# Attention and two feed-forward layers: earlier transposes of two tiles, three warming products, another spread of the feed-forward steps

## The chip, the cores and the metric

One NeuronCore of a Trainium2 chip runs the whole program. The metric is the device time of one execution in microseconds (us). It was taken in three runs of the kernel before; one further execution was recorded by the hardware profiler, and the rows below come from that one.

## The reference

For 2 batches and 12 heads, 448 positions and a head size of 64, the program computes causal attention, lays the heads side by side to 896 tokens of 768 features, and sends these through two feed-forward layers of width 2048:

```python
scores = where(mask, -1e9, q @ k.T / sqrt(64))
attn = exp(scores - max(scores))
attn = attn / (sum(attn) + 1e-9)
x = attn @ v                                   # 896 x 768
h = x @ w_in;  x = (max(h, 0) + alpha * min(h, 0)) @ w_out
h = x @ w2_in
g = where(h >= 1, h, where(h <= -1, 0, (h + 1) ** 2 / 4))
out = g @ w2_out
```

## The kernel before

**Attention.** The 24 head sequences are worked on as 12 pairs, numbered from 0. The 448 rows of scores of each head are cut into three tiles of 128 rows (tile i has 128 * (i + 1) columns, since the mask cuts the rest) and a rest of 64 rows; the rests of both heads share one tile of 128 partitions ("rest tile", index NQ). A pair goes through three periods of a loop over p: in period p the scores, the reductions, the exponentials and the normalization of pair p are issued, the transposes of pair p - 1, and the product with V of pair p - 2. There are 14 periods, so that the last two only finish pairs 10 and 11.

The work of one pair: `scores` (lines 376 and 372) puts products into the PSUM banks s0 and s1 (one for each head) and s2 (rest tile). VectorE reads them (line 383), adds the mask, takes the row's extreme and writes the tile to SBUF. `expo` (line 392) makes the exponentials on ScalarE, in place. `norm` divides: GpSimd adds 1e-9 to the sums (line 399), VectorE takes the reciprocal (line 400), GpSimd multiplies the tiles (line 403), in the order 0, 1, rest, 2. `transp` (line 430) turns 64 x 64 blocks by products with the identity into the PSUM banks t0 and t1, each of which exists twice, so that a third group of transposes has to wait until the first is copied out. The copies to SBUF (line 439) are shared: of tiles 0 to 2 ScalarE copies one head and VectorE the other; of the rest tile VectorE copies both. `attnv` (lines 446 and 454) multiplies with V into the one bank o, from which ScalarE takes a rounded part (`high`, line 213) and VectorE the remainder (`low`, line 216).

**Order.** It is written out by hand: the schedule is the order in which the loop body issues (lines 489 to 529), and each engine works its queue in that order. The banks s0 and s1 exist once: the third tile's scores wait until the first two tiles' scores are read, and the next pair's first scores wait until the third tile's are read.

**Loads.** SyncE's queue issues nearly all transfers in program order: per pair the queries and keys (line 336, 448 KB; those of pair 0 in two halves, one of them on ScalarE's queue, line 334), two small blocks of queries for the rest tile (line 340), and seven pieces of V (line 348). In period 1 two chunks of the first feed-forward weights (line 103, 768 KB each) are issued ahead of the loads for pair 3 that follow in period 2.

**Before the attention.** `warm_up` (line 72) issues NWARM = 9 products of zeros, 512 columns each, into the bank o, one after the other.

**Feed-forward.** Weights come as 64-bit numbers. `Weights.prime` is a generator that splits the first three chunks into two parts of reduced precision, one step at each call: a magnitude on ScalarE (line 113), four steps on VectorE, the last of them with a cast on ScalarE (line 150), a subtraction on VectorE (line 153), and then the next load and magnitude. `early_tiles` is a generator that issues products of the first feed-forward layer (line 253) for tiles of the input that are ready: its ten steps have six products each for the first output tile, three each for the second, over five of the six input tiles; the first output tile uses the banks s0 and s1. `spare(n)` calls both at three places of a period: one step of `prime` at the first place from period 3 on, and in the last two periods one step of `prime` and two steps of `early_tiles` at each place. What is then left of both runs after the loop; the four passes of the feed-forward layers (`run_layer`) follow.

Of the kernel before, what the change touches and what calls it, by code (L numbers as in the profile page):

```python
# [22 lines left out]
def attention_moe_moe_kernel(ctx: ExitStack, tc: tile.TileContext, qk, v, w1, w2, w3, w4, alpha, out):  # L23
# [8 lines left out]
    nc = tc.nc  # L32
# [13 lines left out]
    NM, NC2, _, KC, _ = w2.shape  # L46
    SCALE = 1.0 / float(D) ** 0.5
    MASK = -1e9 / SCALE
    NWARM = 9

    const = ctx.enter_context(tc.tile_pool(name="const", bufs=1))
    xpool = ctx.enter_context(tc.tile_pool(name="x", bufs=1))
# [4 lines left out]
    def f32(t):  # L57
        return t.bitcast(F32)
# [7 lines left out]
    def warm_up():  # L66

        z = const.tile([128, 512], F32R, tag="zero", name="zero")
        nc.vector.memset(f32(z), 0.0)  # L69
        for _ in range(NWARM):  # L70
            ps = ps_o.tile([128, 512], F32, tag="o", name="warm_ps")
            nc.tensor.matmul(ps, lhsT=z[:, :128], rhs=z, start=True, stop=True)  # L72

    def constants():
        nc.vector.memset(half, 0.5)
        make_identity(nc, ident)
        for t, p0, n in ((mask, 0, Q), (mask_rest, 0, D), (mask_rest, D, D)):
            if p0 == 0:
                nc.gpsimd.memset(t, 0.0)
            d = t[p0:p0 + n, t.shape[1] - n:]  # L80
            nc.gpsimd.affine_select(
                out=d, in_=d, compare_op=ALU.is_ge, fill=MASK, base=0, pattern=[[-1, n]], channel_multiplier=1
            )


    class Weights:
# [82 lines left out]
        def next(self):  # L169
            self.n_used += 1  # L170
            return self.split.pop(self.n_used - 1)
# [59 lines left out]
    def interleave(a, b):  # L231
        a, b = list(a), list(b)
        while a or b:
            for ops in (a, b):
                if ops:
                    ops.pop(0)()

    def new_banks():

        pools = (ps_s, "s0"), (ps_s, "s1"), (ps_s, "s2"), (ps_o, "o"), (ps_t, "t0"), (ps_t, "t1"), (ps_t, "t0"), (ps_t, "t1")  # L240
        while True:
            for pool, tag in pools:
                yield pool.tile([128, 512], F32, tag=tag, name="ps")
# [17 lines left out]
    def early_tiles(batches):  # L261

        for f, bs in enumerate(batches):
            ws = wts.next()
            ps = {b: new_tile() for b in bs}
            early[f] = ws, ps
            for k in range(KD - 1):
                products(ps, ws, x_t, k, k, k == 0, False)
                yield
# [35 lines left out]
    class Attention:  # L305
# [101 lines left out]
        def transp(self, p, tiles):  # L407


            ps = [self.ps_t.tile([128, 512], F32, tag=f"t{h}", name=f"t{h}_ps") for h in range(2)]  # L410
            if 0 in tiles:

                self.pt[p] = (
                    self.ap.tile([Q, 2, 2, NQ, NQ * D], F32, tag="pt", name="pt", bufs=2),
                    self.ap.tile([Q, 2, NC, D], F32, tag="pt_rest", name="pt_rest", bufs=2),
                )
            (pt, pt_rest), off, copies = self.pt[p], 0, []
            for i in tiles:
                n = NC if i == NQ else i + 1
                rows = self.rows(p, i)  # L420
                dst = [
                    t[:, off:off + len(rows) * n * D].rearrange("p (j c q) -> p j c q", c=n, q=D) for t in ps
                ]
                off += len(rows) * n * D
                for c in range(n):
                    for j, (e, _) in enumerate(rows):
                        e = self.prest[p % 3] if i == NQ else e
                        for h in range(2):
                            g = slice(h * D, (h + 1) * D)
                            nc.tensor.transpose(dst[h][:, j, c, :], e[g, c * Q:(c + 1) * Q], ident[g, g])  # L430
                if i == NQ:

                    for h in range(2):
                        copies.append((nc.vector.tensor_copy, pt_rest[:, h], dst[h][:, 0]))
                else:
                    for h, copy in enumerate((nc.scalar.copy, nc.vector.tensor_copy)):
                        copies.append((copy, pt[:, h, :, :n, i * D:(i + 1) * D], dst[h]))
            for copy, to, src in copies:
                copy(to, src)  # L439
# [23 lines left out]
    with tc.manual_schedule():  # L463
        wts = Weights()
        ps_s, ps_t, ps_o = (
            ctx.enter_context(tc.tile_pool(name=f"ps_{n}", bufs=b, space=PSUM))
            for n, b in (("s", 1), ("t", 2), ("o", 1))
        )
        banks = new_banks()
        with ExitStack() as pa:  # L470
            ap = pa.enter_context(tc.tile_pool(name="attn", bufs=2))
            at = Attention(ap, ps_s, ps_t, ps_o)
            at.zeros()
            at.load(0)
            warm_up()
            at.load(1)
            at.load_v(0)
            nc.sync.dma_start(out=alpha_sb, in_=alpha)
            constants()
            early = {}  # L480
            fill = early_tiles(((0, 1), (0,)))
            prime = wts.prime()
            PRIME = 3

            for p in range(NP + 2):
                new, mid, old = p < NP, 1 <= p <= NP, p >= 2  # L490

                def spare(n):
                    if p >= PRIME and (n == 0 or not new):
                        next(prime, None)
                    if not new:
                        next(fill, None)
                        next(fill, None)

                if new:
                    at.scores(p, (0, 1))  # L500
                    at.scores(p, (NQ,))
                    at.expo(p, (0, 1, NQ))
                if old:
                    at.attnv(p - 2)
                    high, low = at.evac(p - 2)
                    high()
                spare(0)
                if new:
                    at.scores(p, (2,))
                if mid:  # L510
                    at.transp(p - 1, (0, 1))
                if old:
                    low()
                if new:
                    at.expo(p, (2,))
                spare(2)
                if mid:
                    at.transp(p - 1, (NQ,))
                    at.transp(p - 1, (2,))
                if new:  # L520
                    at.norm(p)
                spare(1)
                if 0 < p < NP - 1:
                    at.load(p + 1)
                if p + 1 < NP:
                    at.load_v(p + 1)
                if p == PRIME - 2:
                    wts.load()
                    wts.load()
            for _ in fill:  # L530
                pass
            for _ in prime:
                pass
        gpool = ctx.enter_context(tc.tile_pool(name="g", bufs=1))
        ep = ctx.enter_context(tc.tile_pool(name="ep", bufs=2))
        late = []
        for layer in (1, 2, 3, 4):
            late = run_layer(layer, late)
            if layer % 2 == 0:
                interleave(late, [])  # L540
                late = []
# [44 lines left out]
```

## Time and profile before

| | us |
|---|---|
| median of 3 runs | 569.93 |
| lowest, highest | 567.62, 570.9 |
| the profiled execution | 569.33 |
| its span in the profile | 567.4 |

Engines in that span: TensorE's products 550.1 us busy (97%), its weight loads 482.7 (85%), VectorE 420.9 (74%), ScalarE 237.8 (42%), GpSimd 136.1 (24%). TensorE's granted clock is 0.996 of full speed in the mean. The span counts from the first instruction to the last; the profiled execution's own time is 1.9 us longer. In the rows PE is TensorE's products, PEld its weight loads, DVE VectorE, ACT ScalarE, POOL GpSimd and SP SyncE; a q behind a name is the queue's sequencer. L376 is line 376 of the kernel. Busy time of TensorE counts overlapping products once and includes the end of the last one, so it says when work was there and not how dense it was.

### The profile page before, as it was taken

The numbers are of one execution on the slowest core, as the hardware profiler recorded it, in microseconds if no ns is written. First come the engines' busy times: TensorE is split into PE (matmuls) and PEld (weight loads), VectorE is DVE, ScalarE is ACT, GpSimd is POOL, SyncE is SP. The second block draws the span as 40 slices with busy tenths as digits, with TensorE's granted clock in tenths as the row PEclk, the third lists the DMA queues.
The fourth block names the chain that finished last, engine by engine and source line by source line (L and its number), as shares of the span: only waits on it lengthen the run. The fifth ranks groups of instructions, "written<-read, shape, count | busy, mean of one in ns | idle before, by whom it ended". The sixth has DMA issues, their size and how long they took to land.

```text
span 567.4 us, 8740 instructions
## 1 busy us (share of the span) xinstructions
PE 550.1 (97%) x3201; PEld 482.7 (85%) x3201; DVE 420.9 (74%) x809; ACT 237.8 (42%) x497; POOL 136.1 (24%) x179
## 2 busy tenths in 40 slices
PE   8888888999999999999999999999999999999997
PEld 3555556899999999999999999999999999999996
DVE  1778874788888899876665868888888867655750
ACT  2777883233333333332332335555555533232220
POOL 2556653033333333000000003333333300000000
PEclk9999998999999999999999999999999999999999
DMA  4643610333333223445233533333332235434421
GB/s 123 216 125 110 183 31 5 109 111 113 112 111 112 93 75 79 145 113 145 102 89 110 166 113 111 112 111 113 111 94 75 75 119 144 137 118 137 143 71 32
DMA packets 25674, 62.31 MB, mean 110 GB/s; under 512 B 5280, under 2 KB 13984, under 8 KB 25632
## 3 DMA queue, kind: packets, MB, share of 16 engines
q1 hardware_dynamic: 23760, 60.15, 33.7%
q10 hardware_dynamic: 1872, 1.61, 0.8%
q8 instruction: 25, 0.41, 0.3%
q14 instruction: 17, 0.14, 0.1%
HBM read 58.99 MB, written 2.75 MB: 109 GB/s over the span
## 4 chain that ended last, share of the span: by engine, by line
PE 95%; DVE 3%; issue 1%; POOL 1%; ACT 0%; ACTq 0%; POOLq 0%
PE ps L253 82%; PE s_ps L376 3%; PE o_ps L446 3%; PE rest_ps L372 2%; DVE pexp L383 2%; PE warm_ps L72 1%; PE t_ps L430 1%; DVE pt L439 1%; PE o_ps L454 1%; POOL pexp L403 0%; ACT pexp L392 0%; POOL prest L403 0%; DVE x L216 0%; DVE stat L383 0%; DVE zero L69 0%
## 5 line engine op out<-in xcount | busy, mean ns | idle before, releaser
L253 PE MATMUL ps<-x,w_split 128*128 128x448 f32 x1152 | 235.0, 366 | 0.0
L253 PE MATMUL ps<-g,w_split 128*128 128x448 f32 x1152 | 233.8, 365 | 0.0
L253 PEld LDWEIGHTS ps<-x,w_split 128*128 128x128 f32 x1152 | 216.1, 188 | 17.6 <-DVE w_split L153 0.4
L253 PEld LDWEIGHTS ps<-g,w_split 128*128 128x128 f32 x1152 | 216.4, 188 | 17.1
L177 POOL TENSOR_TENSOR g<-act_g,g 128x448 fp32r<-128x448 f32 x64 | 85.6, 1338 | 274.1 <-ACT g L176 274.1
L150 ACT CAST w_split<-w_f 128x512 fp32r<-128x512 f32 (+1 forms) x80 | 56.5, 707 | 126.9 <-DVE w_f L147 94.9
L153 DVE TENSOR_TENSOR w_split<-w_f,w_split 128x512 fp32r<-128x512 f32 (+1 forms) x80 | 66.1, 827 | 50.5 <-ACT w_split L150 50.5
L176 ACT CAST g<-act_g 128x448 fp32r<-128x448 f32 x64 | 36.2, 565 | 76.6 <-DVE act_g L189 62.8
L129 DVE TENSOR_SCALAR w_f<-w_f 128x512 f32<-128x512 f32 (+1 forms) x80 | 58.5, 731 | 8.7 <-ACT w_f L113 8.5
L141 DVE SCALAR_TENSOR_TENSOR w_f<-w_raw,w_f 128x512 uint32<-128x512 uint32 (+1 forms) x80 | 63.5, 793 | 1.4
L147 DVE SCALAR_TENSOR_TENSOR w_f<-w_raw,w_f 128x512 uint32<-128x512 uint32 (+1 forms) x80 | 63.5, 793 | 1.4
L113 ACT ACTIVATE w_f<-w_raw 128x512 f32<-128x512 f32 (+1 forms) x80 | 61.2, 765 | 0.5 <-DMA w_raw<-w 0.4
L392 ACT ACTIVATE pexp<-pexp,stat 128x128 f32<-128x128 f32 (+2 forms) x72 | 35.9, 501 | 18.3 <-DVE stat L383 18.3
L383 DVE CUSTOM_DVE_ANT_0 pexp<-s_ps,mask 128x128 f32<-128x128 f32 (+2 forms) x72 | 26.2, 412 | 22.6 <-PE s_ps L376 22.5
L135 DVE TENSOR_SCALAR w_f<-w_f 128x512 uint32<-128x512 uint32 (+1 forms) x80 | 38.2, 478 | 1.4
L201 ACT ACTIVATE act_t<-act_t,half 128x448 f32<-128x448 f32 x32 | 21.5, 672 | 37.7 <-DVE act_t L200 37.7
L403 POOL TENSOR_SCALAR pexp<-pexp,stat 128x128 f32<-128x128 f32 (+2 forms) x72 | 33.9, 489 | 10.6 <-DVE stat L383 7.9
L226 DVE COPY o_sb<-ps 128x224 f32<-128x224 f32 x12 | 4.7, 392 | 29.9 <-ACT o_sb L226 29.9
L430 PEld LDWEIGHTS t_ps<-ident,pexp 64*128 64x128 f32 x288 | 13.5, 138 | 15.2 <-issue 8.4
L430 PE MATMUL t_ps<-ident,pexp 64*128 64x64 f32 x288 | 16.1, 226 | 9.3 <-ACT pt L439 4.9
L376 PE MATMUL s_ps<-qk_raw 64*128 64x128 f32 (+2 forms) x144 | 23.8, 425 | 1.0 <-DVE stat L383 1.0
L446 PEld LDWEIGHTS o_ps<-pt,v 128*64 128x64 f32 x144 | 9.9, 143 | 14.5 <-issue 11.1
(46 smaller groups left out, 288.7 us busy)
## 6 DMA issues: line engine op xcount, KB each, us to landing
w_raw<-w SPq DMA_DIRECT2D x32, 768.0 KB, 4.3
w_raw<-w SPq DMA_DIRECT2D x48, 512.0 KB, 3.7
qk_raw<-qk SPq DMA_DIRECT2D x11, 448.0 KB, 3.9
out<-o_sb SPq DMA_DIRECT2D x12, 112.0 KB, 1.7
out<-o_sb ACTq DMA_DIRECT2D x12, 112.0 KB, 1.7
v<-v SPq DMA_DIRECT2D x12, 56.0 KB, 2.9
v<-v SPq DMA_DIRECT2D x12, 48.0 KB, 2.4
v<-v SPq DMA_DIRECT2D x12, 40.0 KB, 2.0
```

The source lines that it names most:

```text
L113: nc.scalar.activation(out=f32(w), in_=f32(hi), func=AF.Abs)
L129: nc.vector.tensor_scalar(out=f32(w), in0=f32(w), scalar1=HI_MIN, scalar2=HI_MAX, op0=ALU.max, op1=ALU.min)
L135: nc.vector.tensor_scalar(out=w, in0=w, scalar1=5, scalar2=2, op0=ALU.logical_shift_left, op1=ALU.logical_shift_right)
L141: nc.vector.scalar_tensor_tensor(out=w, in0=hi, scalar=0xC0000000, in1=w, op0=ALU.bitwise_and, op1=ALU.bitwise_or)
L147: nc.vector.scalar_tensor_tensor(out=w, in0=lo, scalar=29, in1=w, op0=ALU.logical_shift_right, op1=ALU.bitwise_or)
L150: nc.scalar.copy(s[:, 0, :n], f32(w))
L153: nc.vector.tensor_sub(s[:, 1, :n], f32(w), f32(s[:, 0, :n]))
L176: nc.scalar.copy(t[:, 0, :], g)
L177: nc.gpsimd.tensor_sub(t[:, 1, :], g, f32(t[:, 0, :]))
L253: nc.tensor.matmul(ps[b][:, :S], lhsT=ws[:, part, k * 128:(k + 1) * 128], rhs=src[b, kk][:, xp, :], start=first and part == 0 and xp == 0, ...
L376: nc.tensor.matmul(ps, lhsT=t[h, 0, i * Q:(i + 1) * Q], rhs=t[h, 1, :w], start=True, stop=True)
L383: nc.vector.tensor_tensor_reduce(out=e, in0=ps, in1=m, scale=-SCALE, scalar=3.0e38, op0=ALU.add, op1=ALU.min, accum_out=self.st[p][:, 0, c ...
```

## The change

Three things are edited. NWARM goes from 9 to 3. Of the rest tile's two transposed halves, ScalarE copies one and VectorE the other. The loop body issues the transposes of tiles 0 and 1 ahead of the third tile's scores. `spare` no longer does anything while new pairs come; from period 3 on one step of `prime` is issued at the place where it was before (behind `high`). In the last two periods `spare` makes one step of `prime` and one step of `early_tiles`, and its first call stands ahead of the product with V instead of behind it, so that a period has four steps of `prime` and three of `early_tiles` instead of three and six.

```diff
-    NWARM = 9
+    NWARM = 3
...
                 if i == NQ:
-                    for h in range(2):
-                        copies.append((nc.vector.tensor_copy, pt_rest[:, h], dst[h][:, 0]))
+                    for h, copy in enumerate((nc.scalar.copy, nc.vector.tensor_copy)):
+                        copies.append((copy, pt_rest[:, h], dst[h][:, 0]))
...
-                def spare(n):
-                    if p >= PRIME and (n == 0 or not new):
+                def spare():
+                    if not new:
                         next(prime, None)
-                    if not new:
-                        next(fill, None)
                         next(fill, None)
 
                 if new:
                     at.scores(p, (0, 1))
                     at.scores(p, (NQ,))
                     at.expo(p, (0, 1, NQ))
+                spare()
                 if old:
                     at.attnv(p - 2)
                     high, low = at.evac(p - 2)
                     high()
-                spare(0)
+                if p >= PRIME:
+                    next(prime, None)
+                if mid:
+                    at.transp(p - 1, (0, 1))
                 if new:
                     at.scores(p, (2,))
-                if mid:
-                    at.transp(p - 1, (0, 1))
                 if old:
                     low()
                 if new:
                     at.expo(p, (2,))
-                spare(2)
+                spare()
                 if mid:
                     at.transp(p - 1, (NQ,))
                     at.transp(p - 1, (2,))
                 if new:
                     at.norm(p)
-                spare(1)
+                spare()
```

## Rows read from the trace of the kernel before

**Rows 1.** Windows: stretch, its length, each engine's busy time (instructions), clock, DMA

```profile
103.41:567.40 463.99, 460.45 (x2272) 426.46 (x2271) 352.41 (x543) 171.98 (x277) 85.61 (x64) 1.00 0.34 108
```

**Rows 2.** Chain that ended last (start, us, what): period 2; start of pair 11

```profile
20.84 0.71 PE s_ps L376 x8
21.55 0.95 PE rest_ps L372 x2
22.50 1.45 PE o_ps L446 x12
23.95 0.46 PE o_ps L454 x16
24.41 0.90 PE s_ps L376 x4
25.30 0.54 DVE pexp L383
...
25.85 0.47 DVE pexp L383
...
26.33 0.55 DVE pt L439 x2
...
27.01 0.56 PE t_ps L430 x11
27.57 0.71 PE s_ps L376 x8
...
81.37 0.71 PE s_ps L376 x8
```

**Rows 3.** Timeline of TensorE in period 2: start, us, what; transposes in order

```profile
25.09 0.53 PE L430 MATMUL t_ps<-ident,pexp 64*128 64x64 f32 x12
25.45 0.42 PE L430 MATMUL t_ps<-ident,prest 64*128 64x64 f32 x8
```

**Rows 4.** Windows, one period in the middle; busy PE, PEld, DVE, ACT, POOL

```profile
61.19:67.92 6.73, 5.84 (x78) 3.76 (x77) 5.95 (x23) 5.15 (x18) 4.34 (x9) 1.00 0.70 228
```

**Rows 5.** Timeline of the start, TensorE: warming products, first scores, period 1

```profile
1.86 7.62 PE L72 MATMUL warm_ps<-zero 128*128 128x512 f32 x9 [1.86 <-DVE half L75]
...
9.41 1.65 PE L376 MATMUL s_ps<-qk_raw 64*128 64x128 f32 x8
...
15.32 0.52 PEld L376 LDWEIGHTS s_ps<-qk_raw 64*128 64x128 f32 x6 [0.18 <-DVE stat L383]
...
16.16 0.30 PEld L372 LDWEIGHTS rest_ps<-qk_raw,qdiag 128*128 128x128 f32 x2 [0.33 <-issue]
```

**Rows 6.** The page's costliest groups: the magnitude step on ScalarE

```profile
L113 ACT ACTIVATE w_f<-w_raw 128x512 f32<-128x512 f32 (+1 forms) x80 | 61.2, 765 | 0.5 <-DMA w_raw<-w 0.4
```

**Rows 7.** DMA issues, 0.5 to 1.0 and 18.05 to 18.4 us: KB, us to landing

```profile
qk_raw<-qk ACTq DMA_DIRECT2D x1, 224.0 KB, 3.4
...
qk_raw<-qk SPq DMA_DIRECT2D x1, 448.0 KB, 6.7
```

**Rows 8.** Timeline of SyncE's queue: issues for pairs 3 and 11

```profile
18.07 0.38 SPq L336 DMA_DIRECT2D qk_raw<-qk  x1
...
68.41 0.53 SPq L336 DMA_DIRECT2D qk_raw<-qk  x1
```

**Rows 9.** Windows around 89 us; the number ahead of the last two is the granted clock

```profile
86.00:89.00 3.00, 1.20 (x26) 0.84 (x22) 3.00 (x11) 2.22 (x7) 0.51 (x2) 0.98 0.00 0
89.00:92.00 3.00, 2.80 (x17) 1.78 (x19) 0.98 (x3) 0.00 (x0) 2.67 (x5) 0.50 0.02 5
```

**Rows 10.** Chain that ended last, end of the attention

```profile
86.86 0.53 DVE pt L439 x2
...
89.20 2.83 PE o_ps L446 x12
...
92.68 2.63 PE ps L253 x12
```

**Rows 11.** Timeline of GpSimd, end of the attention

```profile
89.33 2.16 POOL L403 TENSOR_SCALAR pexp<-pexp,stat 128x128 f32<-128x128 f32 x4 [1.02 <-DVE stat L400]
```

## The prediction

> **What bounds the kernel now.** I first cut the span at the end of the attention [rows 1]. Behind 103.41 us lie 464 us in which TensorE is busy 460: the feed-forward products of line 253, which the change leaves as they are. Only the 103 us ahead can move. Next I read the chain of waits over one period of the attention, that of pair 2 (pairs count from 0) [rows 2]: 20.84 to 27.57, 6.73 us; the next pairs repeat it until pair 11 starts at 81.37, so eight periods lie between pair 3 and pair 11. The reader is to see where the chain leaves TensorE: after the third tile's scores (24.41) it goes through VectorE, two reductions (to 26.32) and then the copy of the first two tiles' transposes (0.55), before the last transposes may have their bank (27.01). That copy could have run long before, but stands behind the two reductions in VectorE's queue. The transposes themselves are cheap: twelve go out in 0.36 (25.09 to 25.45) [rows 3]. A later period, cut by engine [rows 4], says how near the others are: of 6.73, TensorE is busy 5.84, VectorE 5.95 with a step of the weights' split in it, ScalarE 5.15, GpSimd 4.34.
>
> **The period.** With the first transposes ahead of the third tile's scores, their copies run while those scores are computed, and the last transposes no longer wait for VectorE. What is late next: the banks of the scores. The next pair's first scores write the two banks that the two reductions read. So the new loop is: scores 0.90, reductions 0.54 and 0.47 (1.91 in all), a hand-over of 0.13 (26.88 to 27.01 in the old chain), then the first scores, whose second head has to wait for the second reduction. How long these take when released so is seen in period 1: the second head's weight loads start at 15.32, the rest tile's at 16.16 [rows 5], 0.84. Then 0.95 of rest scores, 1.45 and 0.46 of attention times V, 0.36 of transposes: 1.91 + 0.13 + 0.84 + 0.95 + 1.91 + 0.36 = 6.10. The gain is 0.63 per period. Bounds: the 5.84 that TensorE is busy at best, 6.73 at worst. I take 6.10, since each term is on the path today.
>
> One copy of the rest tile goes from VectorE to ScalarE; VectorE's queue gets shorter. ScalarE has 1.6 idle per period, which covers it. Where a weight step falls on ScalarE too (0.77 in the mean [rows 6], in two of the eight periods), the cover is nearly used up; I charge 0.2 each, 0.4 (bounds 0 and 1.5, both steps in full). Whether GpSimd's normalizations come in time for the earlier transposes I cannot read to better than half a microsecond; that is rival 2.
>
> **Fewer warming products.** Nine take 7.62 us, 0.85 each [rows 5], since each waits for the one before it in the same bank. Six fewer end 5.1 earlier, at 4.4. The half of pair 0's data that ScalarE's queue issues, before 1.0, lands 3.4 later [rows 7], by 4.4 as well. Pairs 0 to 2 thus start some 5.0 earlier.
>
> What do the six buy? In the rows nothing: the first scores, right behind nine products, take 1.65 for eight where the steady period takes 0.71 [rows 2, 5]. That is TensorE's low level (1.2 GHz). So I cost the removal at zero in clock. The Trainium skill, "TensorE: Matmul & The Clock Gate", section "Why this matters for your kernels", speaks against this edit: it says to warm TensorE up with matmuls ahead of work that is to run at full clock. By that, taking them away keeps the clock low for longer, and the sum below would be 3.6 worse (rival 3); the rows of the first scores do not bear it out.
>
> **What the earlier start runs into.** Pair 3's queries and keys. SyncE's queue issues them at 18.07, behind two weight chunks, and they land 6.7 later, at 24.8 [rows 7, 8]. Nothing that the change touches stands ahead of them in that queue, so 24.8 holds. Pair 3 starts at 27.57 today; 5.0 + 0.6 earlier would be 22.0. So it starts at 24.8, a gain of 2.8 and not 5.6, and TensorE stands idle for nearly 3 us. Later pairs are not held: pair 11's data is issued at 68.41, and even 6.7 more is before my start of pair 11, about 76.
>
> **The clock in that hole.** Near 89 us the trace shows a fall [rows 9]: TensorE was busy 1.20 of the 3 us from 86 to 89, and ran at a granted clock of 0.50 from 89 to 92, where twelve products of attention times V took 2.83 instead of 1.45 [rows 2, 10]. Half of those 3 us and a little behind them was lost, 1.6. A hole of 3 us is longer than that one, so I expect a fall there and charge 1.6 (bounds 0 and 3.2, two such stretches).
>
> **The end of the attention.** Today pair 11 starts at 81.37 and 22.0 later, at 103.41, 33 feed-forward products have gone out in three groups, of which the first takes 2.63 for 12 [rows 10]. In the new order, from the start of pair 11 at t: third-tile scores at t+4.0 (0.71 + 0.95 + 1.91 + 0.36), reductions done at t+5.9. The first six products need the score banks, so they run from t+5.5 to t+6.9 (0.22 each). Attention times V for pair 10 waits for the copies: today it starts 2.34 behind the reductions (86.86 to 89.20); of these the first tiles' copy (0.53) and one of two rest copies (half as much, an estimate) go, so it starts at t+7.4 and at full clock ends at t+9.3. The hole ahead of it is 0.5, with products before it. GpSimd's four normalizations (2.16 [rows 11]) start just then, and hold the next transposes until t+9.7. Then twelve transposes (0.36), six products (1.3), twenty transposes (0.6), twelve products (2.6), attention times V (1.9): t+16.5. By then 24 products are out; nine more at 0.22 make t+18.5, and with 0.4 for hand-overs t+18.9. Gain 3.1, half of it the clock. The weight steps come earlier there; VectorE is busy 0.98 of the 3 us from 89 to 92 [rows 9], which covers them; without it each would cost about its 0.8.
>
> **The sum.** 2.8 for pair 3, minus 1.6 for the clock, plus 8 x 0.63 = 5.0, minus 0.4, plus 3.1: 8.9. The profiled execution took 569.33 (span 567.4 and 1.9 around it), so 560.4; it lies 0.6 below the median of the runs.
>
> **Rivals.**
> 1. No fall of the clock at pair 3, all else as forecast: 1.6 less, 558.8. For it: TensorE waits in every period (6.73 less 5.84), and the clock stays up. Against: this hole is far longer.
> 2. The wait moves instead of going: GpSimd's or ScalarE's queue holds the period at 6.73. Then only 2.8 - 1.6 + 3.1 = 4.3 is left, 565.0. For it: both have little to spare; against: both show idle time now.
> 3. The clock stays low through pairs 1 and 2. TensorE's work doubles there: 2.6 of pair 1's (0.71 + 0.95 + 0.90) lie on the path, and pair 2 takes 11.7 (twice 5.84), so pair 3 starts at 4.4 + 11.4 (9.41 to 20.84) + 2.6 + 11.7 = 30.1 instead of 24.8, with no hole and no fall: 8.9 - 5.3 + 1.6 = 5.2, 564.1. This is what the Trainium skill's page "TensorE: Matmul & The Clock Gate" would lead to (same section).
> 4. Pair 3's data does not hold the start: 5.0 + 9 x 0.63 - 0.4 + 3.1 = 13.4, 555.9. Against: the two weight chunks stand ahead in the same queue.
> 5. Slower: the faster attention outruns SyncE's queue, every pair waits for its data, and the clock falls in each of these holes at 1.6 a fall. With all eight pairs behind pair 3: 12.8 against the gain of 8.9, 573.2; fewer than eight do not make it slower by the 2.8 below. Against: even the last pair's data is there in time.
>
> **How the numbers follow.** Chances: forecast 0.54, the rivals 0.20, 0.14, 0.06, 0.03, 0.03. The range reaches from 557.0 (no fall, and a period of 5.9) to 565.5 (rival 2 and a little), leaving out rivals 4 and 5 and tails. A measurement of this kernel can tell some 0.5%, 2.8 us, from no change. All but the fifth are faster by more than that, but part of rival 2, where the end gains little too, falls within: 0.93 faster, 0.04 same, 0.03 slower.
>
> **What would show it.** First scores near 4.4 and at the low level; a wait of pair 3's scores until about 24.8, and a granted clock of 0.50 behind it; periods near 6.1 whose chain runs from the two reductions to the next first scores, with no copy in it; no fall near the end. I am wrong if pair 3 starts well before 24, if the period stays at 6.7, or if the clock falls more than once.

## The result, and the profile after

The changed kernel took 563.38 us in the median of four runs (562.45 to 563.78) against 569.64 for the kernel before in the same set: ratio 0.9891, 95% interval 0.9859 to 0.9923. That is 6.3 us faster; 560.4 had been forecast, with 557.0 to 565.5 as the range. The profiled execution took 563.78, span 561.9, so against the profiled one of before it is 5.5 us shorter. Executions in a slower state, over 1.5% longer, are left out of all comparisons; the profiled execution of the experiment "spread alone" below is one, and only its first 100 us are read.

TensorE's timeline of the changed kernel (start, us, what; in brackets the idle time before and what ended it):

```profile
1.86 2.50 PE L72 MATMUL warm_ps<-zero 128*128 128x512 f32 x3 [1.86 <-DVE half L75]
4.29 1.65 PE L376 MATMUL s_ps<-qk_raw 64*128 64x128 f32 x8
...
7.66 1.11 PE L376 MATMUL s_ps<-qk_raw 64*128 64x384 f32 x4
...
20.75 0.61 PE L430 MATMUL t_ps<-ident,pexp 64*128 64x64 f32 x12
26.11 1.65 PE L376 MATMUL s_ps<-qk_raw 64*128 64x128 f32 x8 [4.75 <-DMA qk_raw<-qk]
27.69 1.86 PE L372 MATMUL rest_ps<-qk_raw,qdiag 128*128 128x448 f32 x2
29.48 2.74 PE L446 MATMUL o_ps<-pt,v 128*64 128x384 f32 x12
...
35.09 0.90 PE L376 MATMUL s_ps<-qk_raw 64*128 64x128 f32 x8
35.92 1.02 PE L372 MATMUL rest_ps<-qk_raw,qdiag 128*128 128x448 f32 x2
...
39.20 0.86 PE L376 MATMUL s_ps<-qk_raw 64*128 64x384 f32 x4
...
40.15 0.68 PE L430 MATMUL t_ps<-ident,pexp 64*128 64x64 f32 x12
40.72 1.40 PE L376 MATMUL s_ps<-qk_raw 64*128 64x128 f32 x8
42.05 1.02 PE L372 MATMUL rest_ps<-qk_raw,qdiag 128*128 128x448 f32 x2
...
59.30 0.68 PE L430 MATMUL t_ps<-ident,pexp 64*128 64x64 f32 x12 [0.60 <-POOL pexp L403]
...
79.27 1.02 PE L372 MATMUL rest_ps<-qk_raw,qdiag 128*128 128x448 f32 x2
...
84.15 1.50 PE L253 MATMUL ps<-x,w_split 128*128 128x448 f32 x6
86.05 1.52 PE L446 MATMUL o_ps<-pt,v 128*64 128x384 f32 x12 [0.40 <-ACT pt L439]
...
96.06 4.12 PE L253 MATMUL ps<-x,w_split 128*128 128x448 f32 x19
```

The reader is to see four things. The first scores come at 4.29 instead of 9.41, as slow as before (1.65). Pair 3's scores wait 4.75 us for their data, and what follows runs at half speed: the rest tile's two take 1.86, against 1.02 at 35.92. Then the periods are short: from the rest tile's scores of pair 4 (35.92) to those of pair 5 (42.05) are 6.13 us. And at the end the product with V of pair 10 runs at full speed (1.52, where it was 2.83 in [rows 10]), with six feed-forward products ahead of it.

The clock and the queue behind the wait. Windows (stretch, its length, busy PE, PEld, DVE, ACT, POOL, granted clock, DMA share, GB/s):

```profile
21.50:26.00 4.50, 0.00 (x0) 0.00 (x0) 1.68 (x6) 1.74 (x6) 2.97 (x7) 0.91 0.68 250
26.00:32.00 6.00, 5.89 (x22) 2.80 (x24) 1.83 (x10) 2.62 (x10) 0.64 (x2) 0.50 0.44 116
32.00:36.00 4.00, 3.55 (x65) 2.72 (x61) 2.69 (x9) 3.23 (x9) 0.07 (x1) 1.00 0.50 155
```

Its DMA issues from 18.05 to 18.5 us (KB, us to landing):

```profile
qk_raw<-qk SPq DMA_DIRECT2D x1, 448.0 KB, 7.9
```

TensorE did nothing from 21.5 to 26. Its clock fell before the wait ended (0.91 in the mean of that stretch) and stayed at half until about 32. Pair 3's queries and keys were issued at 18.09, as before (18.07 in [rows 8]), and took 7.9 to land instead of 6.7.

### The profile page after: what moved, and what is told of

Same layout as the page of the kernel before. It is cut to its first block, busy times and chain, and to the rows that moved or that the text cites. A ratio compares the mean times of both kernels' runs of the same rounds, so it can differ in the third digit from the quotient of the medians.

```text
span 561.9 us, 8739 instructions
## 1 busy us (share of the span) xinstructions
PE 547.4 (97%) x3195; PEld 482.2 (86%) x3195; DVE 418.4 (74%) x797; ACT 240.6 (43%) x509; POOL 136.6 (24%) x179
## 4 chain that ended last, share of the span: by engine, by line
PE 84%; POOL 0%; DVE 0%; ACT 0%; issue 0%; ACTq 0%
PE ps L253 83%; PE o_ps L446 0%; PE t_ps L430 0%; POOL pexp L403 0%; PE o_ps L454 0%; DVE o_sb L226 0%; ACT o_sb L226 0%; ACTq L226 0%
## 5 line engine op out<-in xcount | busy, mean ns | idle before, releaser
L201 ACT ACTIVATE act_t<-act_t,half 128x448 f32<-128x448 f32 x32 | 21.5, 672 | 37.7 <-DVE act_t L200 37.7
L376 PE MATMUL s_ps<-qk_raw 64*128 64x128 f32 (+2 forms) x144 | 25.4, 431 | 5.6 <-DMA qk_raw<-qk 4.8
L439 DVE COPY pt<-t_ps 128x128 f32<-128x128 f32 (+2 forms) x36 | 14.0, 418 | 13.1 <-PE t_ps L430 13.1
L200 DVE TENSOR_SCALAR act_t<-ps 128x448 f32<-128x448 f32 x32 | 19.9, 622 | 3.0 <-PE ps L253 2.4
```

## The experiments

The change has four edits, counting the rest tile's copy; the experiments take them apart. The ratios are against the kernel before, whose runs fall on two levels: mostly 567.2 to 567.6 where the mean granted clock is 1.000, and 569.0 to 570.0 where it is 0.996 or 0.997. The profiled execution, with its fall near 89 us, is one of the second kind; where the clock fell in the others is not on record, and a few near 569.9 have 1.000 too. Beside each ratio stand the medians themselves, to be held against 563.4.

**Nine warming products.** In the changed kernel:

```diff
-    NWARM = 3
+    NWARM = 9
```

> The changed kernel with nine warming products again (its other edits stay). Theory (the earlier start runs into the data of pair 3, and the hole there drops the clock): pair 3 starts at about 26.9, right after its data lands, without a hole and at full clock; pair 4 starts at about 33 instead of 35.1, and the time is about 561.3, 2 us FASTER than the changed kernel with three. Rival (leaving out six products is worth the 5.1 us that they take): 568.5. Rival (the products are worth nothing either way): 563.4.

Measured: 561.91 (561.45 to 563.52), ratio 0.9886 (0.9864 to 0.9908). TensorE's timeline:

```profile
25.30 0.64 PE L430 MATMUL t_ps<-ident,pexp 64*128 64x64 f32 x12
25.88 1.40 PE L376 MATMUL s_ps<-qk_raw 64*128 64x128 f32 x8
...
32.78 0.90 PE L376 MATMUL s_ps<-qk_raw 64*128 64x128 f32 x8
```

Pair 3 starts at 25.88 right behind the transposes, with no wait, and pair 4 at 32.78, 2.3 ahead of the changed kernel; the profiled spans differ by as much (559.6 against 561.9). The medians differ by 1.5, and the runs overlap: the slowest with nine (563.52) lies above two of those with three. With the other edits in place, leaving out six warming products certainly does not gain the 5.1 us that they take, and more likely makes the kernel slower than faster.

**Six.** The same line with 6:

```diff
-    NWARM = 3
+    NWARM = 6
```

> The changed kernel with six warming products instead of three and nothing else. Theory: pair 3 would be ready at 24.6 and its data lands at 25 to 26, so the hole shrinks from 4.8 to 1 to 2 us; pair 3 starts when it does with three products, the clock stays up, pair 4 starts at 31.5 to 32.2, and the time is 560 to 561. Rival (a hole of this length drops the clock as well): 562 to 563.4.

Measured: 561.72 (560.81 to 562.62), ratio 0.9892 (0.9873 to 0.9910). TensorE's timeline of the profiled execution (561.06):

```profile
26.17 0.93 PE L376 MATMUL s_ps<-qk_raw 64*128 64x128 f32 x8 [1.96 <-DMA qk_raw<-qk]
...
32.37 0.90 PE L376 MATMUL s_ps<-qk_raw 64*128 64x128 f32 x8
```

Pair 3 starts when it does with three (26.17 against 26.11), since its data sets that; but here the clock stayed up and the period took 6.2 instead of 9.0. Both answers occur: three runs have a mean granted clock of 0.999 and took 560.8 to 561.1, three have 0.996 and took 562.4 to 562.6. One fall costs 1.6. (Where it fell in those three is not on record; pair 3's wait is the likely place.)

**The hole filled.** In the changed kernel, twenty products of zeros ahead of pair 3's scores; their result is not used:

```diff
+    def dense(n):
+        ps = ps_o.tile([128, 512], F32, tag="o", name="dense_ps")
+        for _ in range(n):
+            nc.tensor.matmul(ps, lhsT=z[:, :128], rhs=z, start=True, stop=True)
...
+                if p == PRIME:
+                    dense(20)
                 if new:
                     at.scores(p, (0, 1))
```

> The changed kernel with twenty products of zeros, one behind the other without waits, ahead of pair 3's scores (their result is not used). They fill some 4.3 us of the hole. Theory (the hole costs twice, as a wait and by the clock): pair 3 still waits for its data, but the clock stays up, period 3 takes 6.1 instead of 9.0, and the time is about 560.5. Rival (the clock is not what made period 3 long, or products of zeros do not hold it): 563.4.

Measured: 561.91 (561.77 to 561.97), ratio 0.9881 (0.9860 to 0.9903), a mean granted clock of 1.000 in all five runs. TensorE's timeline (the new function moves the scores to line 382):

```profile
22.28 4.83 PE L71 MATMUL dense_ps<-zero 128*128 128x512 f32 x20 [0.98 <-DVE x L222]
27.04 0.93 PE L382 MATMUL s_ps<-qk_raw 64*128 64x128 f32 x8
...
33.23 0.90 PE L382 MATMUL s_ps<-qk_raw 64*128 64x128 f32 x8
```

The products last longer than the wait and put pair 3 off by 0.9, and the kernel is still 1.5 faster: the period takes 6.2. So the clock, and not the wait alone, made that period long. The runs also lie within 0.2 of each other, where those of the other versions spread by 0.8 to 4. Falls make part of that spread, as in "six", but not all of it: the runs of "nine" differ by 2.1 at mean clocks of 0.999 and 1.000, and for that no cause was found.

**The weights behind pair 3.** In the changed kernel:

```diff
                 if 0 < p < NP - 1:
                     at.load(p + 1)
+                if p == PRIME - 1:
+                    wts.load()
+                    wts.load()
                 if p + 1 < NP:
                     at.load_v(p + 1)
-                if p == PRIME - 2:
-                    wts.load()
-                    wts.load()
```

> The changed kernel with the two first weight chunks issued one period later, behind the queries and keys of pair 3. Theory: pair 3's data lands at about 21.5, pair 3 starts at about 22 with no hole; pair 4's data (issued at the same place as now) lands at 29.5 to 30.5, which leaves a hole of about 2 us there; pair 4 starts at 30.5 instead of 35.1, and the time is 558.8 without a fall of the clock and 560.5 with one. Rival (SyncE's queue is not what holds pair 3, or the magnitude on ScalarE now waits for the weights and takes its place): 563.

Measured: 561.03 (560.50 to 562.45), ratio 0.9864 (0.9839 to 0.9888). TensorE's timeline:

```profile
21.58 1.40 PE L376 MATMUL s_ps<-qk_raw 64*128 64x128 f32 x8
...
30.79 1.65 PE L376 MATMUL s_ps<-qk_raw 64*128 64x128 f32 x8 [2.14 <-DMA qk_raw<-qk]
```

Pair 3 no longer waits: the two chunks ahead of it in SyncE's queue were its wait. The wait turns up at pair 4, shorter (2.14), and the clock falls there. The gain is 2.4 where the forecast had 3 to 4.6.

**One chunk behind pair 3, one behind pair 5.**

```diff
-                if p == PRIME - 2:
-                    wts.load()
-                    wts.load()
...
+                if p in (PRIME - 1, PRIME + 1):
+                    wts.load()
```

> The changed kernel with the first weight chunk issued behind the queries and keys of pair 3 and the second two periods later, behind those of pair 5. Theory (SyncE's queue and the two chunks in a row are what makes the hole): pair 3 starts at about 22, pair 4's data lands near 28.5, no wait is longer than 1 us, the clock stays up, pair 4 starts at 28.5 to 29 instead of 35.1, and the time is 557 to 558. Rival (a hole opens at pair 4 or 5 and the clock falls there): 559.5 to 561.

Measured: 561.10 (560.55 to 564.67), ratio 0.9879 (0.9848 to 0.9911): near the rival. TensorE's timeline of the profiled execution, the slowest of the six (564.67):

```profile
70.41 1.65 PE L376 MATMUL s_ps<-qk_raw 64*128 64x128 f32 x8 [1.85 <-DMA qk_raw<-qk]
```

Spreading the chunks spreads the wait: here pair 10 waits behind the third chunk, and there the clock falls; pairs 5 and 7 had waited for their data before, 1.17 and 0.76. The other five runs took 560.55 to 561.66, with mean clocks of 0.996 to 1.000. That a faster attention has to meet SyncE's queue somewhere is not shown: in the profiled executions of "nine" and of the kernel with six products and the weights behind (below), waits named for queries and keys stay within 0.3 us.

**Three warming products alone.** In the kernel before:

```diff
-    NWARM = 9
+    NWARM = 3
```

> The kernel before with three warming products and nothing else changed. Theory: pairs 0 to 2 come 5 us earlier, pair 3 waits for its data until 25 to 26, the clock falls there for one or two stretches, pair 4 starts at 34 to 35.5 where it started at 34.1; the time is 568.5 to 571, no change. Rival (the earlier start is kept): 564.5.

Measured: 568.49 (567.70 to 570.07), ratio 0.9999 (0.9984 to 1.0014). TensorE's timeline:

```profile
26.39 1.65 PE L376 MATMUL s_ps<-qk_raw 64*128 64x128 f32 x8 [3.90 <-DMA qk_raw<-qk]
...
35.91 0.90 PE L376 MATMUL s_ps<-qk_raw 64*128 64x128 f32 x8
...
91.02 1.52 PE L446 MATMUL o_ps<-pt,v 128*64 128x384 f32 x12 [1.10 <-DVE stat L400]
```

Worth nothing by itself. Pairs 0 to 2 come five microseconds earlier, pair 3 one, and pair 4 starts at 35.91, 1.8 later than in the timeline of the kernel before (34.10). The span is nearly the same (567.7 against 567.4), because the end is shorter: the same wait of 1.10 ahead of pair 10's product with V came without a fall here (1.52, where before took 2.83 [rows 10]).

**The order alone.** In the kernel before, the transposes of tiles 0 and 1 ahead of the third tile's scores:

```diff
+                if mid:
+                    at.transp(p - 1, (0, 1))
                 if new:
                     at.scores(p, (2,))
-                if mid:
-                    at.transp(p - 1, (0, 1))
```

> The kernel before with the transposes of tiles 0 and 1 ahead of the third tile's scores and nothing else changed (nine warming products, both rest copies on VectorE, the feed-forward steps as before). Theory: the period falls from 6.73 to 6.1 to 6.2, pair 11 starts at 75 to 76 instead of 81.4, the end of the attention stays as long as it was (22), and the time is 563 to 564. Rival (without the rest copy on ScalarE or the other spread, VectorE's queue takes the wait over): period 6.5 or more, 567 or more.

Measured: 566.06 (563.82 to 566.11), ratio 0.9950 (0.9930 to 0.9970), between the two answers; the two runs with a mean clock of 1.000 took 563.8 and 563.9, as the theory said. TensorE's timeline:

```profile
71.31 0.68 PE L430 MATMUL t_ps<-ident,pexp 64*128 64x64 f32 x12 [1.01 <-POOL pexp L403]
...
78.76 1.02 PE L372 MATMUL rest_ps<-qk_raw,qdiag 128*128 128x448 f32 x2
...
85.80 2.36 PE L446 MATMUL o_ps<-pt,v 128*64 128x384 f32 x12 [1.72 <-DVE stat L400]
```

Five of the nine periods from pair 2 to pair 11 are 6.13, four are 6.3 to 6.7: there the last transposes wait. The row at 71.31 names GpSimd, but its normalization had ended at 70.32. What ended just ahead of the transposes, at 71.22, is ScalarE's copy of the first two tiles, which has to be out of their bank, and which stood behind a weight step on ScalarE (0.92 from 69.87). It is the same in three of the four long periods; in the fourth (6.33) it is GpSimd. Pair 11's rest scores start at 78.76, 3.3 ahead of before (82.01). The end then takes as long as it did, both with a fall: 21.3 from there until 33 feed-forward products are out, though the wait for the copies is longer (1.72 against 1.10). Seven of the nine runs have a mean clock of 0.996 or 0.997.

**The rest copies on VectorE.** In the changed kernel:

```diff
-                    for h, copy in enumerate((nc.scalar.copy, nc.vector.tensor_copy)):
-                        copies.append((copy, pt_rest[:, h], dst[h][:, 0]))
+                    for h in range(2):
+                        copies.append((nc.vector.tensor_copy, pt_rest[:, h], dst[h][:, 0]))
```

> The changed kernel with both copies of the rest tile on VectorE again. Theory (the move of that copy is worth little, since the period runs through the reductions and the next first scores): period 6.13 as now, 563 to 563.8. Rival (it lies on the path by way of the reciprocal or the last copy): period 6.4, 565.5.

Measured: 564.71 (564.33 to 565.23), ratio 0.9936 (0.9913 to 0.9958): 1.3 slower than the changed kernel, between the two answers. From its timelines, with those of the changed kernel first:

```profile
67.55 0.40 ACT L392 ACTIVATE pexp<-pexp,stat 128x128 f32<-128x128 f32 x1 [0.20 <-DVE stat L383]
...
70.38 0.92 ACT L113 ACTIVATE w_f<-w_raw 128x768 f32<-128x768 f32 x1
...
71.20 0.51 ACT L439 COPY pt<-t_ps 128x128 f32<-128x128 f32 x2
...
71.82 0.68 PE L430 MATMUL t_ps<-ident,pexp 64*128 64x64 f32 x12 [0.67 <-issue]
```

With both copies on VectorE:

```profile
67.64 0.40 ACT L392 ACTIVATE pexp<-pexp,stat 128x128 f32<-128x128 f32 x1 [0.80 <-DVE stat L383]
...
69.77 1.15 POOL L403 TENSOR_SCALAR pexp<-pexp,stat 128x384 f32<-128x384 f32 x2
...
71.28 0.53 ACT L439 COPY pt<-t_ps 128x128 f32<-128x128 f32 x2
...
71.90 0.68 PE L430 MATMUL t_ps<-ident,pexp 64*128 64x64 f32 x12 [1.00 <-POOL pexp L403]
```

The last row names GpSimd, but its normalization had ended at 70.92; ScalarE's copy of the first two tiles ended at 71.81, just ahead of the transposes, behind the same weight step as in the changed kernel (70.47 here). This period takes 6.71, against 6.39 in the changed kernel. The difference begins in VectorE's queue: behind two rest copies the third tile's copy and the next pair's reductions come later, so that ScalarE waits 0.80 for the first of these instead of 0.20. Counted from the rest tile's scores its exponentials start 0.33 later, and its copy of the first tiles with them. The seven periods to pair 11 take 44.03 instead of 43.35, and the end 0.3 more. The edit that I had costed at a charge of 0.4 is a gain.

**The spread alone.** In the kernel before:

```diff
-                def spare(n):
-                    if p >= PRIME and (n == 0 or not new):
+                def spare():
+                    if not new:
                         next(prime, None)
-                    if not new:
-                        next(fill, None)
                         next(fill, None)
...
+                spare()
                 if old:
                     at.attnv(p - 2)
                     high, low = at.evac(p - 2)
                     high()
-                spare(0)
+                if p >= PRIME:
+                    next(prime, None)
```

(and `spare()` for the other two calls.)

> The kernel before with the new spread of the feed-forward steps over the last two periods and nothing else changed. Theory: periods stay at 6.73, the six products ahead of the product with V of pair 10 fill its wait, the clock stays up near 89, and the end of the attention is 2 to 3 us shorter: 566.5 to 567. Rival (the fall comes all the same, or the products only move): 569.

Measured: 566.62 to 567.33 in three runs, ratio 0.9966 (0.9939 to 0.9994). TensorE's timeline:

```profile
87.66 1.49 PE L253 MATMUL ps<-x,w_split 128*128 128x448 f32 x6
89.08 1.52 PE L446 MATMUL o_ps<-pt,v 128*64 128x384 f32 x12
```

The six products take the place of the wait, and the clock stays up in each of the three runs (1.000). Against runs of before with a clock of 0.996 or 0.997 that is 2 to 3 us, against those with 1.000 about half a microsecond. So this edit mostly buys certainty about the clock; three runs alone would not show that, but of the 15 runs of "nine", "the hole filled" and the kernel with six products and the weights behind, which all have this spread, none has a mean clock below 0.999.

**Dense warming.** In the kernel before:

```diff
-    NWARM = 9
+    NWARM = 18
...
+        ps = ps_o.tile([128, 512], F32, tag="o", name="warm_ps")
         for _ in range(NWARM):
-            ps = ps_o.tile([128, 512], F32, tag="o", name="warm_ps")
             nc.tensor.matmul(ps, lhsT=z[:, :128], rhs=z, start=True, stop=True)
```

> The kernel before with eighteen warming products in one go into the bank, without the wait for one another that the nine have; nothing else changed. Theory (the nine leave TensorE waiting half of the time, and that is why the clock does not rise in them): the clock rises before the first scores, these take 0.7 to 0.9 for eight instead of 1.65 and start at 6 to 8 instead of 9.4; pair 3 then meets its data at 25, and the time is 567 to 568.5. Rival (products of zeros do not raise the clock at all): eighteen take 7.7, the first scores come at 9.5 and take 1.65, the time is unchanged.

Measured: 568.25 (567.30 to 569.58), ratio 1.0002 (0.9985 to 1.0019). TensorE's timeline:

```profile
1.86 6.50 PE L72 MATMUL warm_ps<-zero 128*128 128x512 f32 x18 [1.86 <-DVE half L75]
8.29 0.93 PE L376 MATMUL s_ps<-qk_raw 64*128 64x128 f32 x8
...
25.84 0.93 PE L376 MATMUL s_ps<-qk_raw 64*128 64x128 f32 x8 [0.99 <-DMA qk_raw<-qk]
26.70 1.72 PE L372 MATMUL rest_ps<-qk_raw,qdiag 128*128 128x448 f32 x2
```

Eighteen products that don't wait for one another, in 6.50 us, do bring the clock up where nine spaced ones in 7.62 did not: the first scores take 0.93 instead of 1.65. (Their number changed with their spacing; no run took the two apart.) The time is unchanged all the same, because pair 3 meets its data, and the clock falls behind a wait of 0.99.

**Two versions meant to beat both kernels.** The weights behind pair 3 (the edit above) with `NWARM = 6`:

> The changed kernel with six warming products, and with the two first weight chunks behind the queries and keys of pair 3. Theory (what the early start is worth is set by when the data of pairs 3 and 4 lands): pair 3 starts at about 24.7 (its data is there at 20.5), pair 4 at about 30.8, when its data lands, so that no hole is long enough for a fall; the time is 559 to 560, better than all so far. Rival (a later pair waits in SyncE's queue and the clock falls there): 561 to 562.

Measured: 560.90 (560.51 to 561.27), ratio 0.9877 (0.9858 to 0.9897), the lowest median of all that ran, but only 0.1 us below "weights behind pair 3", whose runs overlap with its own, and every run below the changed kernel's fastest (562.45). No run shows a fall, but the time lies between the two answers: the start was slower than expected. TensorE's timeline:

```profile
6.85 1.65 PE L376 MATMUL s_ps<-qk_raw 64*128 64x128 f32 x8
...
17.07 1.60 PE L376 MATMUL s_ps<-qk_raw 64*128 64x384 f32 x4
...
23.93 0.86 PE L376 MATMUL s_ps<-qk_raw 64*128 64x384 f32 x4
```

The clock was still low at 17.07 (1.60 for what later takes 0.86), where the changed kernel's had risen during pair 0's third tile (1.11 at 7.66). And the same with eighteen dense warming products:

> The changed kernel with eighteen warming products in one go instead of three spaced ones, and with the two first weight chunks behind the queries and keys of pair 3. Theory (the clock has to be up before the first scores, and the start has to meet the data of pairs 3 and 4): the clock rises at 6 to 7, the first scores take 0.9 at 8.3, pair 3 starts at about 24 (its data is there at 20.5 to 21), pair 4 at 30.1 to 30.5 when its data lands, no hole, no fall; the rest tile's scores of pair 4 start at 31.1 where the changed kernel with six products and the same loads had 33.2, and the time is 558.8 to 559.5, the best of all. Rival (a later pair waits for its data and the clock falls): 560.5 to 562.

Measured: 561.69 (560.59 to 563.78), ratio 0.9886 (0.9857 to 0.9915): no better. TensorE's timeline:

```profile
29.35 0.68 PE L430 MATMUL t_ps<-ident,pexp 64*128 64x64 f32 x12 [0.68 <-issue]
30.94 0.93 PE L376 MATMUL s_ps<-qk_raw 64*128 64x128 f32 x8 [0.91 <-DVE pt L439]
31.79 1.66 PE L372 MATMUL rest_ps<-qk_raw,qdiag 128*128 128x448 f32 x2
```

The start was quick, and pair 4 met its data again: a wait of 0.68 and one of 0.91 next to each other, and a fall (1.66 for the rest tile). The row of the second wait names VectorE's copy, but the scores need pair 4's queries and keys, and these landed at 30.76 (issued at 27.46, 3.3 to landing). Three of the six runs have a mean clock of 0.997.

## Why the prediction was right, and where its sum was off

The forecast had 8.9 us of gain, the two profiled executions differ by 5.5. The time alone does not tell why: 563.4 lies nearer to rival 3's 564.1 than to the 560.4 of the forecast. The trace does: the first scores at 4.29 and low, the wait at pair 3 and the clock of 0.50 behind it, periods of 6.13 and no fall near the end are all as forecast. Term by term:

- **Pair 3's start: 2.8 forecast, 1.3 measured.** The mechanism was right: the data decides, at the place and in the queue that the prediction named, and "weights behind pair 3" shows that the two chunks are the cause. The landing was mis-sized: "so 24.8 holds". The issue time held (18.09), the transfer did not: 7.9 us instead of 6.7, and the first scores come at 26.11, against 27.4 before. In the other runs that leave the queue as it is, the wait ends between 25.8 and 26.4. Issued at about the same time, the transfer took 7.1 with nine products in the changed kernel, 7.7 with six and in "dense warming", 7.9 with three. Why it is longer there is not settled: from 20 to 22 us the transfers move 421 GB/s before and 415 after, so the sum of them is not slower.
- **The clock in the hole: a charge of 1.6, measured 2.9** (26.11 to 35.09 is 8.98, less a period of 6.13); with the hole filled the same period took 6.2. The step that missed is "charge 1.6 (bounds 0 and 3.2, two such stretches)": it is nearly the far bound that came, 0.50 over 6 us. In three of the four runs the mean granted clock is 0.993; the one at 0.996 is also the fastest, 562.45. "Six" puts the price of one stretch at 1.6, as taken from before.
- **The period: 6.10 forecast, 6.13 measured** where nothing else holds it; "I take 6.10, since each term is on the path today" was right. The chain of terms is seen at 39.20 to 40.72: the third tile's scores, the last transposes without a wait, then the next first scores, drawn out to 1.40 because their second head waits for the second reduction. From pair 4 to pair 11 (35.92 to 79.27) seven periods take 43.35, two of them 6.31 and 6.39. My 0.4 for ScalarE's cover comes out at 0.44, in two periods in which a weight step stands on ScalarE, as forecast: its copy of the first two tiles ends at 59.20 and 71.71, a tenth ahead of the last transposes. (The row at 59.30 names GpSimd, which had ended a little earlier, at 59.07.) What was wrong is the reason: I charged it to the moved rest copy, but with that copy back on VectorE the same two periods take 6.44 and 6.71. Rival 2's ScalarE queue thus holds two periods, for a quarter of a microsecond.
- **The rest copy: forecast as a small cost, measured as a gain of about one.** The prediction looked at the queue that the copy went to and called the one it left merely shorter. What is behind it in that queue are the next pair's reductions, which ScalarE's exponentials wait for.
- **The end of the attention: 3.1 forecast, 2.6 measured.** From pair 11's rest scores to 33 products out: 21.3 before (82.01 to 103.34); now 79.27 to 96.06 with 24 out and nine more at 0.2, so 98.0, 18.7. The wait for the copies is 0.40 (0.5 forecast). "Half of it the clock" holds: "three alone", with the old spread and no fall, took 19.9 for this stretch (83.83 to 103.69), so 1.5 are the clock and 1.1 the spread.

So 1.3 - 2.9 + 4.3 + 2.6 = 5.3 in place of 8.9, against the 5.5 measured (the 4.3 is seven periods, 3.7, and 0.6 of pair 3's own). The miss lies in the first two terms, both at pair 3. In the prediction's own sums, rival 3 is 3.7 worse than the forecast (564.1 against 560.4), not 3.6.

On the rivals: rival 3, a clock that stays low through pairs 1 and 2, did not come in the changed kernel (pair 0's third tile already took 1.11 where the low level takes 1.60), but in the profiled run of "six, weights behind" it was low through pairs 0 and 1 (until after 18.45 us). The Trainium skill, "TensorE: Matmul & The Clock Gate", "Why this matters for your kernels", says for benchmarks to warm up with matmuls first, since otherwise the low clock is measured. "Dense warming" agrees with that (0.93 for the first eight scores); behind the nine spaced products of the kernel before they took 1.65 all the same. Rival 4 did not come: the data held pair 3. Of rival 5 the mechanism exists (an attention that meets SyncE's queue, and falls there), but in the changed kernel once and not at each pair.

The prediction set its sum against one execution with a fall near 89 us. Runs of before at 567.2 to 567.6, with a mean clock of 1.000, are 2 us faster, so a part of the forecast gain was there for the executions with the fall alone: against the faster ones the change gains 4, not 6.3.

## What to carry to other kernels

Before a start-up is shortened, look where the earlier work meets the next thing that does not move with it, here a transfer behind two larger ones in the same queue: the time saved is what lies between, less what the wait does to TensorE's clock. Time gained ahead of such a wait can be worth less than nothing; nine, six or three warming products then differ mainly in whether the clock falls in the wait. When a copy moves between queues, ask what stands behind it in the queue that it leaves. And where a row names what ended a wait, see whether that work ended just ahead of it: GpSimd, named at 71.90 above, had been done for one microsecond.

## What the runs showed of the hardware that was not expected

- Products of zeros bring up the clock when they don't wait for one another: behind eighteen such, 6.50 us in all, the first eight scores take 0.93; behind nine that wait for one another, 7.62 us in all, 1.65. Twenty dense ones also held it where TensorE otherwise waited for nearly five microseconds (1.000 in all five runs).
- Whether a short wait drops the clock differs from run to run of one kernel: of the six runs of "six" three have a mean clock of 0.999, among them the profiled one with a wait of 1.96 at pair 3, and three have 0.996. "Dense warming" fell behind 0.99. And the same wait of 1.10 at the end of the attention came with a fall in the profile of before and without one in that of "three alone". The first rise varies as well: during pair 0 in the changed kernel, at the start of pair 2 with six products and the weights behind.
- The same 448 KB, issued at the same time behind the same two chunks, landed after 6.7 in the kernel before and after 7.9 in the changed one; with the chunks issued behind it, in "weights behind pair 3", it took 3.5.
